# Linear attention and a SwiGLU layer on one core: tokens dealt in runs of five and four, v cast by DMA, another order in the prologue

## The chip, the cores and the metric

The kernel runs on one core of a Trainium2 chip. The metric is device time in microseconds, and lower is better. TensorE (PE in the profile, PEld for its weight loads) multiplies matrices; VectorE (DVE), ScalarE (ACT) and GpSimd (POOL) do the elementwise work; SyncE (SP) only issues transfers. DMAs go out on the queues of SP (q1 in the profile), ACT (q10) and POOL (q0). Only those of POOL change the type on the way, here from float32 to bfloat16. PSUM is the memory that matmuls write; DVE and ACT copy results out of it.

## The reference, cut to what matters

There are 8 batches of 8 heads, 576 tokens and a head dimension of 64.

```python
kv  = einsum('bhsd,bhse->bhde', k, v)
out = einsum('bhsd,bhde->bhse', q, kv)
a   = out / sqrt(mean(out*out, -1) + 1e-6) * g_norm
x   = a.transpose(0, 2, 1, 3).reshape(4608, 512)
xn  = x / sqrt(mean(x*x, -1) + 1e-6) * rms_g
y   = (silu(xn @ w_gate) * (xn @ w_val)) @ w_out     # 512 -> 1536 -> 512
```

## The kernel before, in words

**Tokens.** The 576 tokens of a batch are cut into 512 "main" tokens and 64 "remainder" tokens (`REM`). Main token `4p + c` lies on partition `p`, in chunk `c` (0 to 3, `NC = 4`). The remainder is a chunk number 4 of its own, on partitions 0 to 63 only. So q, k and v of a batch each take a main load (`load_main`, 1 MB, 128 partitions, pieces of 1024 bytes) and a remainder load (`load_rem`, 128 KB, 64 partitions, pieces of 256 bytes), and each is cast to bfloat16 in a main part (`cast_main`, two halves of heads, H0 and H1) and a remainder part (`cast_rem`, tiles `remq`, `remk`, `remv`). The remainder tokens of all batches are gathered in `xr` and go through the feed-forward layer last, as a ninth group. Heads go in pairs `j` (0 to 3, `NS = 4`), two heads filling 128 rows; P0 is pairs 0 and 1, P1 is pairs 2 and 3.

**Attention.** `kv_mm` or `kv_pairs` (L237, L247) accumulates k-transpose times v over the five chunks; `kv_out` copies it to `kvs`. `qT_mm` (L267) transposes q on TensorE and `qT_out` (L277) copies it out to `qTs` (batches 0 and 1); later batches do it by DMA (`qT_dma`). `oT_mm` (L324) and `sqT_` (L335) give the squared output transposed, and `stat_pairs` or `stat_mm` (L343, L353) its sums. `chain` is a row of twelve small DVE instructions (L381 to L399) that folds both norms into one factor per token and head; `xna_` (L307, L409) applies it, `xT_mm` (L426) transposes the result on TensorE, and `xT_out` copies it out as `x`, by turns on DVE (L438) and ACT (L436).

**Feed-forward.** For a group `g`, `slots_a` makes a "gate" and a "val" slot for each of 12 columns `j` of `d_ff` (L536, four matmuls of 128x512 each), and `slots_b` makes 16 slots of three matmuls (L558) for the output projection. Batch 0 uses `slots_b_by_j`, with four PSUM tiles open at once. `store` copies the result out of PSUM (`osb`, L575) and writes it to HBM.

**Order.** Each engine executes its instructions in the order in which the program emits them. `Placer` hands the attention work of the next batch to the slots of the batch before it: `put` takes the first slot from a given one on in which a table of room per engine (`ROOM`, `BEHIND`) is not overrun, and an operation whose input is made by another engine goes at least one slot later. In `emit`, a slot's work for the other engines comes ahead of its matmuls, and its attention matmuls behind them. Slots are numbered from the gate of column 6 of batch 0: 0 to 11 are the rest of `slots_a(0)`, 12 to 27 the "all" slots of `slots_b_by_j(0)`, and 28 to 33 are six empty ones, which hold only what the planner puts there; batch 1's feed-forward begins at slot 34. Attention of batch 1 is placed from slot 10 on, its kv first, then its qT.

**Prologue.** Batch 0's attention is written out by hand. v comes by casting DMAs of POOL in three pieces; k on SP and q on ACT in halves of heads; the three remainders on ACT and SP, behind them. The weight loads on POOL have a manual dependence on the first v load. Batch 1's loads on SP are held until the third `wg` load has landed, and batch 2's until the last `wo` load has. The tile framework orders two engines that read the same PSUM tile one behind the other.

The functions that the diff touches, with the profile's line numbers:

Of the kernel before, what the change touches and what calls it, by code (L numbers as in the profile page):

```python
# [80 lines left out]
def kernel(  # L81
# [32 lines left out]
    rstage = pool("rstage", 4)  # L114
# [17 lines left out]
    gcol = consts.tile([128, 1], FP32, name="gcol")  # L132
    rmsg = consts.tile([128, NS], FP32, name="rmsg")
# [11 lines left out]
    for t in range(3):  # L145
        nc.vector.memset(rems[t][0][REM:], 0.0)
    nc.vector.memset(kvs[0], 0.0)
# [6 lines left out]
    staged, rstaged = {}, {}  # L154
    mains, xs = {}, {}

    def load_main(b, t, heads=(0, H), cs=(0, NC), queue=nc.sync):
        if (b, t) not in staged:
            staged[b, t] = stage.tile([128, H, NC * D], FP32, name="stg")
        h0, h1 = heads  # L160
        view = src[t][b, :, 0:MAIN, :].rearrange("h (p c) d -> p h (c d)", c=NC)
        return queue.dma_start(  # L162
            out=staged[b, t][:, h0:h1, cs[0] * D : cs[1] * D], in_=view[:, h0:h1, cs[0] * D : cs[1] * D]
        )

    def by_head(t):
        if (0, t) not in mains:
            mains[0, t] = qkv.tile([128, NC, H, D], BF16, name=f"main_{'qkv'[t]}")
        return mains[0, t].rearrange("p c h d -> p (c h d)").rearrange("p (h x) -> p h x", h=H)

    def load_cast(t, heads):
        h0, h1 = heads
        view = src[t][0, :, 0:MAIN, :].rearrange("h (p c) d -> p h (c d)", c=NC)
        return nc.gpsimd.dma_start(out=by_head(t)[:, h0:h1], in_=view[:, h0:h1])

    def load_rem(b, t, queue=nc.sync):
        rstaged[b, t] = rstage.tile([REM, H, D], FP32, name="rstg")
        return queue.dma_start(out=rstaged[b, t], in_=src[t][b, :, MAIN:S, :].rearrange("h p d -> p h d"))

    def cast_main(b, t, eng, heads=(0, H), cs=(0, NC)):  # L180
        if (b, t) not in mains:
            mains[b, t] = qkv.tile([128, NC, H, D], BF16, name=f"main_{'qkv'[t]}")
        h0, h1 = heads
        copy = eng.copy if eng is nc.scalar else eng.tensor_copy
        copy(  # L185
            out=mains[b, t][:, cs[0] : cs[1], h0:h1, :],
            in_=staged[b, t].rearrange("p h (c d) -> p c h d", c=NC)[:, cs[0] : cs[1], h0:h1, :],
        )

    def cast_rem(b, t, eng):  # L190
        copy = eng.copy if eng is nc.scalar else eng.tensor_copy
        copy(out=rems[t][b % 2][:REM], in_=rstaged[b, t])

    def load_all(b):
        first = None
        for t in (0, 1, 2):
            i = load_main(b, t)
            first = first or i
        for t in (0, 1, 2):
            load_rem(b, t)  # L200
        return first
# [11 lines left out]
    class Att:  # L213
        def __init__(self, b):
            self.b = b
            self.kv, self.qT = kvs[b % 2], qTs[b % 2]
            self.o, self.outa, self.sq = {}, {}, {}
# [3 lines left out]
        def chunk(self, t, c):  # L221
            if c == NC:
                return rems[t][self.b % 2]
            if self.b == 0 and t == 2:
                return by_head(t).rearrange("p h (c d) -> p c h d", c=NC)[:, c]
            return mains[self.b, t][:, c]
# [46 lines left out]
        def qT_out(self, ps, js, c0, eng):  # L273
            copy = eng.copy if eng is nc.scalar else eng.tensor_copy
            n = ps.shape[2] // 128
            to = self.qT[:, c0 : c0 + n, js[0] : js[-1] + 1, :].rearrange("p c j t -> p j c t")
# [8 lines left out]
        def o_mm(self, c, pool=None):  # L285
            self.o[c] = o = (pool or att_p).tile([128, H, D], FP32, name={None: "att"}.get(pool, "mm1" if pool is mm1_p else "o2"))
            for j in range(NS):
                nc.tensor.matmul(  # L288
                    o[:, 2 * j : 2 * j + 2, :], lhsT=self.qT[:, c, j, :], rhs=self.kv[:, j, :, :],
# [3 lines left out]
        def o_pairs(self, js, c0, c1, pool, name):  # L293
            o = pool.tile([128, c1 - c0, 2 * len(js), D], FP32, name=name)
            for n, c in enumerate(range(c0, c1)):
                for i, j in enumerate(js):
                    nc.tensor.matmul(
                        o[:, n, 2 * i : 2 * i + 2, :], lhsT=self.qT[:, c, j, :], rhs=self.kv[:, j, :, :],
# [21 lines left out]
        def oT_mm(self, js, c0, c1, pool=None):  # L320

            ps = (pool or att_p).tile([128, len(js), (c1 - c0) * 128], FP32, name="o2" if pool else "att")
            for n, j in enumerate(js):
                nc.tensor.matmul(  # L324
                    ps[:, n], lhsT=self.kv[:, j], rhs=self.qT[:, c0:c1, j, :],
# [87 lines left out]
        def x_to(self):  # L413
            if self.b not in xs:
                xs[self.b] = x_p.tile([128, NC, NS, 128], BF16, name="x")
# [16 lines left out]
        def xT_out(self, j, chunks, eng):  # L432
# [9 lines left out]
            if chunks[0] < NC:  # L442
                copy(
                    out=self.x_to()[:, chunks[0] : chunks[-1] + 1, j, :],
# [27 lines left out]
    def place_attention(P, b, casts=(), at=0, chain_at=0, by_pe=False):  # L472
# [7 lines left out]
        p0 = P.psum(0.57, lambda: a.kv_mm((0, 1)), casts)  # L480
        p1 = P.reads(P.put("PE", 0.57, lambda: a.kv_mm((2, 3)), [p0], at=p0[1]))
        kv = [P.reads(P.put("DVE", 0.4, lambda h=h: a.kv_out(h, V), [p1])) for h in range(2)]
        ps = {}
        if by_pe:
            qt = []
            for j in range(NS):
                p = P.psum(0.29, lambda j=j: ps.__setitem__(j, a.qT_mm((j,), N1)), casts)
                eng = ("DVE", V) if j % 2 == 0 else ("ACT", A)
                qt.append(P.reads(P.put(eng[0], 0.67, lambda j=j, e=eng[1]: a.qT_out(ps[j], (j,), 0, e), [p])))
        outs = {}  # L490
# [38 lines left out]
    def x_of(g, s, c0, c1):  # L529
        return xs[g][:, c0 // 128 : c1 // 128, s, :] if g < B else xr[:, s, c0:c1]  # L530
# [31 lines left out]
    def rows_of(g, t):  # L562

        if g < B:
            view = out[g * S : g * S + MAIN, :].rearrange("(p c) d -> p c d", c=NC)
            return [(slice(0, 128), view[:, t, :])]
        return [
            (slice(n * REM, (n + 1) * REM), out[b * S + MAIN : (b + 1) * S, :])
            for n, b in enumerate((2 * t, 2 * t + 1))
        ]  # L570
# [33 lines left out]
    def slots_b_by_j(g):  # L604
# [4 lines left out]
        def part(n):  # L609
# [6 lines left out]
            if n == 4 * PARTS - 1:  # L616
                for t in range(4):
                    store(g, t, box[t], nc.scalar if t % 2 else nc.vector)
# [18 lines left out]
    v_load = [load_cast(2, hsx) for hsx in (H0, (4, 6), (6, 8))][0]  # L637
    load_main(0, 1, H0)
    load_main(0, 0, H0, queue=A)
    load_main(0, 1, H1)  # L640
    load_rem(0, 1, A)
    load_main(0, 0, H1, queue=A)
    load_rem(0, 2, A)
    load_rem(0, 0)
    A.preload_act_table(ACT.Silu)
    with nc.allow_non_contiguous_dma(reason="one column of gains"):
        for half in range(2):
            nc.sync.dma_start(out=gcol[half * D : (half + 1) * D], in_=g_norm.rearrange("(d o) -> d o", o=1))
        nc.sync.dma_start(out=rmsg, in_=moe_rms_g.rearrange("(s p) -> p s", p=128))
    nc.sync.dma_start(out=gbc, in_=g_norm.partition_broadcast(128))  # L650

    make_identity(nc, ident)
    w_loads = [load_w(n) for n in range(len(FB))]
    tc.add_manual_dep(w_loads[0][0].ins, v_load.ins.name, SYNC, reason="the first batch comes first")
    for t in range(3):
        G.memset(rems[t][1][REM:], 0.0)
    G.memset(kvs[1], 0.0)
# [10 lines left out]
    cast_rem(0, 1, V)  # L668
    cast_rem(0, 2, V)
    ps = a.qT_mm(P0, range(NC))  # L670
    a.qT_out(ps[:, 0:1], (0,), 0, A)
    a.qT_out(ps[:, 1:2], (1,), 0, V)
    kva = a.kv_pairs(P0)
    a.kv_pairs_out(kva, P0, 0, V)
    a.kv_pairs_out(kva, P0, 1, A)
    cast_main(0, 0, A, H1)
    cast_main(0, 1, V, H1)
    ps = a.qT_mm(P1, range(NC))
    a.qT_out(ps[:, 1:2], (3,), 0, V)
    t0 = a.oT_mm((0,), 0, NC, o2_p)  # L680
    a.sqT_(t0, (0,), 0, NC)
    a.qT_out(ps[:, 0:1], (2,), 0, A)
    t1 = a.oT_mm((1,), 0, NC, o2_p)
    cast_rem(0, 0, V)
    a.sqT_(t1, (1,), 0, NC)
    ps = a.qT_mm(ALL, (NC,))
    a.qT_out(ps, ALL, NC, A)
# [3 lines left out]
    for j in ALL:  # L691
        V.scalar_tensor_tensor(
            out=gain[:, j : j + 1], in0=rmsg[:, j : j + 1], scalar=float(d_model) ** 0.5, in1=gcol,
# [127 lines left out]
```

## Time and profile before

| what | value |
|---|---|
| median of 3 runs | 347.32 us (346.94 to 347.33) |
| the profiled execution | 346.48 us, of which the span is 344.7 us |
| busy PE, DVE, ACT, POOL | 317.0, 177.3, 136.2, 101.9 us |
| instructions | 4872 |
| DMA moved | 49.38 MB in 77336 packets, 43392 of them under 512 bytes |
| HBM read, written | 37.78 MB, 9.44 MB |

The profile is one execution. It lists busy time by engine and by groups of instructions, what ended each wait, the chain of work that ended last, a timeline, and busy time by chosen stretches. A matmul's busy time holds the latency of its result, so that neighbours overlap; the pace is read from their starts. In rows of stretches the count of instructions stands in brackets, and the last columns are the granted TensorE clock (1.00 is full), the busy share of the DMA engines and the bytes written by DMA in GB/s. A casting DMA counts there with its bfloat16 bytes.

### The profile page before, as it was taken

To read this page: it belongs to the slowest core of one execution; us is meant where nothing else is said; L and a number is where in the kernel's file an instruction comes from. 1 tells how busy PE (TensorE), PEld (TensorE's weight loads), DVE (VectorE), ACT (ScalarE), POOL (GpSimd) and SP (SyncE) were. 2 spreads that over 40 slices of the span, in tenths; PEclk is the share of its full clock that TensorE was granted. 3 is DMA by queue.
4 is the path that set the end of the run, shared out by engine and by line. 5 is a ranking of instruction groups with operands and counts; after the bars stand their busy time and mean duration, and the time that the engine had idled before them with its cause. 6 is when DMAs were issued, how large, how long until landed. Compare 5 with 4: busy or idle time off the path is not lost.

```text
span 344.7 us, 4872 instructions
## 1 busy us (share of the span) xinstructions
PE 317.0 (92%) x1776; PEld 159.0 (46%) x1776; DVE 177.3 (51%) x381; ACT 136.2 (40%) x247; POOL 101.9 (30%) x118
## 2 busy tenths in 40 slices
PE   1187999969899999999999999999999999999993
PEld 1155646545344544554455445444544444444441
DVE  2236534466993678076817671965296423303310
ACT  1142333425953742274228323732473233223321
POOL 3711913503920590068007700860150000000000
PEclk9999999969999999999999999999999999999999
DMA  8999989179606890698259645954200510020013
GB/s 220 212 205 310 242 141 368 32 192 341 132 8 160 281 224 21 164 330 167 48 150 335 139 75 156 350 92 99 91 2 1 128 65 0 0 108 16 0 32 92
DMA packets 77336, 49.38 MB, mean 143 GB/s; under 512 B 43392, under 2 KB 72832, under 8 KB 77312
## 3 DMA queue, kind: packets, MB, share of 16 engines
q1 hardware_dynamic: 69200, 42.38, 44.9%
q0 software_dynamic: 5840, 5.24, 9.5%
q10 hardware_dynamic: 2272, 1.44, 1.5%
q8 instruction: 14, 0.23, 0.3%
q14 instruction: 10, 0.08, 0.1%
HBM read 37.78 MB, written 9.44 MB: 137 GB/s over the span
## 4 chain that ended last, share of the span: by engine, by line
PE 85%; DVE 6%; DMA 4%; ACT 2%; issue 1%; ACTq 1%; POOL 0%; DVEq 0%
PE mm L536 52%; PE o L558 24%; DMA rstg<-in_v_dram 3%; PE att L237 3%; PE att L288 2%; PE mm L558 1%; DVE st L364 1%; DVE xna L409 1%; PE att L324 1%; DVE wg L663 1%; DVE h L553 1%; ACT sqT L335 1%; PE att L267 1%; DMA out_dram<-osb 1%; ACTq L162 0%
## 5 line engine op out<-in xcount | busy, mean ns | idle before, releaser
L553 DVE TENSOR_TENSOR h<-silu,mm 128x512 bf16<-128x512 bf16 (+1 forms) x111 | 74.3, 670 | 80.5 <-PE mm L536 69.8
L547 ACT ACTIVATE silu<-mm 128x512 bf16<-128x512 f32 (+1 forms) x111 | 65.1, 587 | 96.0 <-PE mm L536 85.0
L536 PE MATMUL mm<-x,wg 128*128 128x512 bf16 (+1 forms) x396 | 101.1, 377 | 1.1 <-DVE h L553 1.1
L536 PE MATMUL mm<-x,wv 128*128 128x512 bf16 (+1 forms) x396 | 99.5, 374 | 0.0
L558 PE MATMUL o<-wo,h 128*128 128x512 bf16 x408 | 92.6, 379 | 0.0
L536 PEld LDWEIGHTS <-wg 128*128 128x128 bf16 x444 | 43.7, 99 | 51.7 <-issue 2.7
L359 POOL TENSOR_TENSOR sq<-sq,g 128x512 bf16<-128x512 bf16 x30 | 34.4, 1153 | 101.6 <-ACT sq L314 101.4
L558 PEld LDWEIGHTS <-h 128*128 128x128 bf16 x432 | 41.7, 98 | 47.8 <-DVE h L553 0.2
L536 PEld LDWEIGHTS <-wv 128*128 128x128 bf16 x444 | 42.5, 98 | 44.6 <-issue 0.3
L575 ACT COPY osb<-o 128x512 f32<-128x512 f32 x32 | 18.8, 587 | 72.1 <-PE o L558 72.1
L364 DVE TENSOR_REDUCE st<-sq 128x8 f32<-128x512 bf16 x60 | 38.4, 677 | 0.0
L261 DVE CAST kvs<-att 64x256 bf16<-64x256 f32 x14 | 5.9, 421 | 40.7 <-PE att L237 40.6
L185 POOL CAST main_q<-stg 128x1024 bf16<-128x1024 f32 x14 | 14.4, 1040 | 40.7 <-DMA stg<-in_q_dram 24.5
L409 DVE TENSOR_TENSOR xna<-outa,al 128x512 bf16<-128x512 bf16 x35 | 21.8, 684 | 0.0
L318 ACT CAST outa<-att 128x512 bf16<-128x512 f32 x32 | 19.0, 594 | 0.9 <-PE att L288 0.9
L314 ACT ACTIVATE sq<-att 128x512 bf16<-128x512 f32 x30 | 18.2, 606 | 0.0
L185 POOL CAST main_k<-stg 128x1024 bf16<-128x1024 f32 x14 | 14.3, 1043 | 2.7 <-PE att L324 2.0
L185 POOL CAST main_v<-stg 128x1024 bf16<-128x1024 f32 x14 | 14.2, 1047 | 1.6 <-DMA stg<-in_v_dram 1.6
L536 PE MATMUL mm<-xr,wv 128*128 128x512 bf16 x48 | 12.3, 379 | 0.0
L536 PE MATMUL mm<-xr,wg 128*128 128x512 bf16 x48 | 12.3, 379 | 0.0
L288 PEld LDWEIGHTS <-qTs 128*128 128x128 bf16 x140 | 9.7, 98 | 5.3
L267 PE MATMUL att<-ident,main_q 128*128 128x128 bf16 x32 | 3.5, 265 | 8.9 <-DVE main_q L185 7.1
(96 smaller groups left out, 179.4 us busy)
## 6 DMA issues: line engine op xcount, KB each, us to landing
out_dram<-osb SPq DMA_DIRECT2D x32, 256.0 KB, 2.5
stg<-in_q_dram SPq DMA_DIRECT2D x7, 1024.0 KB, 6.5
stg<-in_k_dram SPq DMA_DIRECT2D x7, 1024.0 KB, 9.0
stg<-in_v_dram SPq DMA_DIRECT2D x7, 1024.0 KB, 11.9
wo<-in_moe_w_out_dram POOLq DMA_DIRECT2D x4, 384.0 KB, 7.4
stg<-in_k_dram SPq DMA_DIRECT2D x2, 512.0 KB, 6.5
stg<-in_q_dram ACTq DMA_DIRECT2D x2, 512.0 KB, 8.6
rstg<-in_q_dram SPq DMA_DIRECT2D x8, 128.0 KB, 10.3
```

Source lines behind the costliest of these rows:

```text
L185: copy(out=mains[b, t][:, cs[0] : cs[1], h0:h1, :], in_=staged[b, t].rearrange("p h (c d) -> p c h d", c=NC)[:, cs[0] : cs[1], h0:h1, :],)
L288: nc.tensor.matmul(o[:, 2 * j : 2 * j + 2, :], lhsT=self.qT[:, c, j, :], rhs=self.kv[:, j, :, :], start=j == 0, stop=j == NS - 1, skip_gro ...
L314: nc.scalar.activation(out=self.sq[c][:, 0], in_=self.o[c], func=ACT.Square)
L318: (eng.tensor_copy if eng else nc.scalar.copy)(out=self.outa[c], in_=self.o[c])
L359: eng.tensor_tensor(out=self.sq[c][:, 1], in0=self.sq[c][:, 0], in1=g2, op=OP.mult)
L364: nc.vector.reduce_sum(out=self.st[:, which, c, :], in_=self.sq[c][:, which], axis=AX.X)
L409: eng.tensor_tensor(out=self.xna[:, c], in0=src, in1=self.al[:, c, :].to_broadcast([128, H, D]), op=OP.mult)
L536: nc.tensor.matmul(ps[:, : c1 - c0], lhsT=w[n][:, s, jj * 128 : (jj + 1) * 128], rhs=x_of(g, s, c0, c1), start=s == 0, stop=s == NS - 1)
L547: nc.scalar.activation(out=si, in_=g_ps, func=ACT.Silu)
L553: nc.vector.tensor_tensor(out=hs[g, j][:, c0:c1], in0=box["silu"], in1=v_ps, op=OP.mult)
L558: nc.tensor.matmul(ps, lhsT=hs[g, j][:, t * 128 : (t + 1) * 128], rhs=wo[j // OB][:, j % OB, :], start=j == 0, stop=j == NF - 1)
L575: (eng.copy if eng is nc.scalar else eng.tensor_copy)(out=o, in_=ps)
```

## The change

Tokens are now dealt otherwise. A batch's 576 tokens go in 128 runs: partition `p` below 64 takes the five tokens from `9p` on, partition `64 + p` the four that follow. The fifth token of the lower half is chunk 4. So one tile holds main and remainder, and each load is two DMAs, one for each half of the partitions (pieces of 1280 and 1024 bytes); the remainder loads and their tiles are gone. `rows_of` follows: a store of batches 0 to 7 is two DMAs of 64 partitions, where it was one of 128. v of batches 0 and 1 goes by casting DMA into a tile `v01`. The prologue does P0 up to its squares before it casts the second half of the heads. The gain vectors come as rows, in three small DMAs on ACT's queue, and are transposed on TensorE. The weight loads no longer wait for the v load. `qTs` of batches 0 and 1 is stored by head pair. Attention of batch 1 is placed from slot 3 on, qT first, kv from slot 9, and the empty slots are two. Batch 3's loads and casts are asked for six slots later, and the four copies of `slots_b_by_j`'s store are all ACT's. The core of the diff:

```diff
+    v01 = consts.tile([128, H, (NC + 1) * D], BF16, name="v01")
...
-    for t in range(3):
+    for t in range(2):
         nc.vector.memset(rems[t][0][REM:], 0.0)
+    nc.vector.memset(v01[REM:, :, NC * D :], 0.0)
...
+    def runs(t, b, heads):
+        view = src[t][b].rearrange("h (p r) d -> p h r d", r=2 * NC + 1)[:, heads[0] : heads[1]]
+        return view[:, :, 0 : NC + 1], view[:, :, NC + 1 :]
+
+    def load(b, t, heads=(0, H), queue=nc.sync):
...
+        for n, of in enumerate(runs(t, b, heads)):
+            to = staged[b, t][n * REM : (n + 1) * REM, heads[0] : heads[1], : of.shape[2] * D]
+            i = queue.dma_start(out=to, in_=of.rearrange("p h r d -> p h (r d)"))
...
+    def load_v01(b, heads=(0, H)):
+        for n, of in enumerate(runs(2, b, heads)):
+            to = v01[n * REM : (n + 1) * REM, heads[0] : heads[1], : of.shape[2] * D]
+            nc.gpsimd.dma_start(out=to, in_=of.rearrange("p h r d -> p h (r d)"))
...
     def load_all(b):
...
+        return [load(b, t) for t in range(3 if b > 1 else 2)][0]
...
+            if b < 2:
+                self.qTj = self.qT.rearrange("p c j t -> p (c j t)").rearrange("p (j c t) -> p j c t", j=NS, c=NC + 1)
...
-                xs[self.b] = x_p.tile([128, NC, NS, 128], BF16, name="x")
+                x = x_p.tile([128, NC, NS, 128], BF16, name="x")
+                if self.b < 2:
+                    x = x.rearrange("p c j t -> p (c j t)").rearrange("p (j c t) -> p c j t", j=NS, c=NC)
+                xs[self.b] = x
...
-                    out=self.x_to()[:, chunks[0] : chunks[-1] + 1, j, :],
+                    out=self.x_to()[:, j, chunks[0] : chunks[-1] + 1, :],
...
+        return xs[g][:, s, cs, :] if g < 2 else xs[g][:, cs, s, :]
...
-    v_load = [load_cast(2, hsx) for hsx in (H0, (4, 6), (6, 8))][0]
...
+    for hsx in (H0, H1):
+        load_v01(0, hsx)
+    load(0, 1, H0)
+    load(0, 0, H0, queue=A)
+    load(0, 1, H1)
+    load(0, 0, H1, queue=A)
     A.preload_act_table(ACT.Silu)
...
     make_identity(nc, ident)
+    make_identity(nc, identf)
     w_loads = [load_w(n) for n in range(len(FB))]
-    tc.add_manual_dep(w_loads[0][0].ins, v_load.ins.name, SYNC, reason="the first batch comes first")
     for t in range(3):
         G.memset(rems[t][1][REM:], 0.0)
+        if t:
+            G.memset(rems[t][0][REM:], 0.0)
     G.memset(kvs[1], 0.0)
...
     cast_main(0, 0, V, H0)
     cast_main(0, 1, V, H0)
-    cast_rem(0, 1, V)
-    cast_rem(0, 2, V)
+    cast_rem(0, 0, V, H0)
+    cast_rem(0, 1, V, H0)
     ps = a.qT_mm(P0, range(NC))
     a.qT_out(ps[:, 0:1], (0,), 0, A)
     a.qT_out(ps[:, 1:2], (1,), 0, V)
+    ps = a.qT_mm(P0, (NC,))
+    a.qT_out(ps, P0, NC, A)
     kva = a.kv_pairs(P0)
     a.kv_pairs_out(kva, P0, 0, V)
-    a.kv_pairs_out(kva, P0, 1, A)
+    a.kv_pairs_out(kva, P0, 1, V)
+    for j in P0:
+        tj = a.oT_mm((j,), 0, NC, o2_p)
+        a.sqT_(tj, (j,), 0, NC)
+    cast_main(0, 1, V, H1)
     cast_main(0, 0, A, H1)
-    cast_main(0, 1, V, H1)
+    cast_rem(0, 1, V, H1)
+    cast_rem(0, 0, V, H1)
     ps = a.qT_mm(P1, range(NC))
...
+    a.qT_out(ps[:, 0:1], (2,), 0, A)
     a.qT_out(ps[:, 1:2], (3,), 0, V)
...
+    ps = a.qT_mm(P1, (NC,))
+    a.qT_out(ps, P1, NC, A)
+    gT = o2_p.tile([128, NS + 1], FP32, name="o2")
+    nc.tensor.matmul(gT, lhsT=grow, rhs=identf, is_transpose=True, start=True, stop=True, skip_group_check=True)
+    V.tensor_copy(out=gall, in_=gT)
...
         V.tensor_tensor(out=sel[rows, 1, half : half + 1], in0=gcol[rows], in1=gcol[rows], op=OP.mult)
-    for j in ALL:
-        V.scalar_tensor_tensor(
...
+    V.tensor_scalar(
+        out=gain, in0=gall[:, 0:NS], scalar1=gcol, scalar2=float(d_model) ** 0.5, op0=OP.mult, op1=OP.mult
+    )
...
+    load_v01(1)
+    wo_loads = [load_wo(n) for n in range(NF // OB)]
...
-                    store(g, t, box[t], nc.scalar if t % 2 else nc.vector)
+                    store(g, t, box[t], nc.scalar)
...
-    slots += [Slot("all", lambda: None) for _ in range(6)]
+    slots += [Slot("all", lambda: None) for _ in range(2)]
...
-            end = place_attention(P, b, casts, 10, by_pe=True)
+            end = place_attention(P, b, casts, 3, by_pe=True, kv_at=9)
...
-            P.put("SP", 0.0, lambda b=b: load_all(b + 1), at=starts[b - 1])
-            casts = place_casts(P, b + 1, starts[b - 1] + 5)
+            P.put("SP", 0.0, lambda b=b: load_all(b + 1), at=starts[b - 1] + 6 * (b == 2))
+            casts = place_casts(P, b + 1, starts[b - 1] + 5 + 6 * (b == 2))
```

## The prediction

> **What bounds the kernel now.** The page comes first: PE is busy 317.0 of 344.7 us. The windows say where it is not. Columns: the stretch, its length, busy time of PE, PEld, DVE, ACT and POOL, granted clock, DMA share, GB/s.
>
> ```profile
> 0.00:14.80 14.80, 1.62 (x12) 1.30 (x13) 3.45 (x12) 1.87 (x2) 7.08 (x15) 1.00 1.00 219
> 14.80:36.00 21.20, 16.32 (x131) 11.63 (x131) 11.35 (x38) 8.75 (x19) 6.04 (x9) 1.00 1.18 261
> ...
> 65.00:77.00 12.00, 8.74 (x69) 5.09 (x68) 9.08 (x28) 2.86 (x6) 1.16 (x3) 0.73 0.52 138
> 77.00:100.40 23.40, 22.28 (x124) 10.94 (x123) 19.84 (x37) 15.87 (x31) 13.44 (x14) 0.99 0.62 178
> ...
> 133.70:167.00 33.30, 33.30 (x185) 16.34 (x184) 19.88 (x41) 14.27 (x26) 13.25 (x14) 1.00 0.65 175
> ```
>
> From 100 us on PE has no gap, so nothing there can be won; only a new wait could show. Time lies in the prologue, between 65 and 77 us, and a little (1.1 us) up to 100 us. The chain of waits names the prologue's first stretch:
>
> ```profile
> 3.18 11.07 DMA rstg<-in_v_dram
> 14.28 0.48 DVE remv L192
> 14.81 0.81 PE mm L247 x6
> 16.25 1.05 ACT main_q L185
> 17.34 1.03 PE att L267 x8
> ```
>
> v's remainder, last in ACT's queue, lands at 14.28; P0's kv, begun at 10.54 when v H0 landed, stands until then. The second stretch is the end of batch 1's attention, in the timelines of PE and, under it, of DVE:
>
> ```profile
> 65.22 0.64 PE L353 MATMUL att<-sel,sqT 128*128 128x4 bf16 x20
> 67.88 0.59 PE L558 MATMUL mm<-wo,h 128*128 128x512 bf16 x2
> 71.44 1.03 PE L426 MATMUL att<-ident,xna 128*128 128x128 bf16 x8 [1.57 <-DVE xna L409]
> 75.27 1.91 PE L536 MATMUL mm<-x,wg 128*128 128x512 bf16 x4
> ```
>
> ```profile
> 68.90 0.69 DVE L409 TENSOR_TENSOR xna<-outa,al 128x512 bf16<-128x512 bf16 x1
> 69.51 0.68 DVE L575 COPY osb<-o 128x512 f32<-128x512 f32 x1
> 70.11 0.68 DVE L575 COPY osb<-mm 128x512 f32<-128x512 f32 x1
> 70.71 1.88 DVE L409 TENSOR_TENSOR xna<-outa,al 128x512 bf16<-128x512 bf16 x3
> ```
>
> After the sums (L353) PE has four slots of output projection left, and is out of work at 68.5; chain, two `osb` copies, `xna` and the copies of x follow each other, and x is whole at 75.77, with PE at half clock.
>
> **Prologue, loads.** Let L be when v H0 is whole. Before, 10.54, in the same place at the head of POOL's queue. By then 2.35 MB had been written, 0.26 MB of them v H0: other queues took most of the traffic, so L in the changed kernel may be as late as when all of q and k (2.36 MB) and v H0 (0.30 MB in bfloat16) are in, 2.66 MB from 2.2 us on. What rate? Rows of the DMA by stretches (length, granted clock, DMA share, GB/s):
>
> ```profile
> 12.00:13.00 1.00, 1.00 1.45 208
> 32.00:34.00 2.00, 1.00 1.09 387
> 60.00:64.00 4.00, 1.00 0.45 88
> ```
>
> Mains on 128 partitions reach 387 GB/s (L = 9.1); a stretch of remainders, 64 partitions in 256-byte pieces, shows 88 (L = 32). The new loads have 64 partitions and big pieces. Rows between are nearer: 2.0 to 10.5 us, the mix of mains and remainders, had 283 GB/s (L = 11.6), and 7 to 13 us, where remainders and the gains' 4-byte pieces weighed most, 241 (L = 13.2). I take their mean, L = 12.4. What goes (24 remainder loads, 640 four-byte pieces) speaks for faster, what comes (every load on half the partitions) for slower.
>
> The page "SBUF — State Buffer" of the Trainium skill, section "Door 1: The DMA port swizzle", speaks against the change: 64 partitions reach half of the ports, 196 GB/s measured against 328, and two DMAs, one for each half, bring 6% more. By it an estimate of L would be 15.8 and the total some 3.4 us above my forecast; no row here shows big pieces on 64 partitions.
>
> **Prologue, from L to the chain.** Ten kv matmuls at this cold stretch's pitch of 0.11, 1.2 us with the last one's latency; two `kvs` copies, both DVE's, 0.28 each, 0.6; `oT` 0.6; two squares on ACT 1.1; then, queued behind them on ACT, the cast of q H1, 1.05; eight transposes 1.05; `qTs` on ACT 0.6 and on DVE 0.4 (one PSUM tile, so one after the other); the gains' copy, `sel` and `gain`, small DVE instructions, 0.75; two `kvs` copies 0.45. With a tenth for hand-overs, `oT` of pair 2 starts at L + 7.9. Before it started at 21.18, and what follows up to the chain (3.78 us, to 24.96) is the same instructions. So the break-even is L = 13.3, and L = 12.4 saves 0.9. k's remainder cast and v's are no more on this path; the halves of k and q land ahead of v H0 and hide behind it.
>
> A floor: `remk`'s zeros are written once more by POOL, and kv's fifth chunk reads them. POOL has four v issues (0.78 each) from 1.26, two identities (0.6), six weight issues (0.77) and three memsets (0.52) before: 11.7, as if L were 11.3. With the memset row of 1.24 us (L657's neighbour at 15.75) it is nearer 12. If the new memset of `v01` on DVE also holds the first v issue, up to 0.6 more. So the prologue saves at most 2.0.
>
> Weights: not held by v any more, but behind it in the same queue, so they start when v H1 ends, at about 13 to 16 us where it was 14; `wg`, `wv` of columns 3 to 5 are needed at 37, of column 6 at 42, and the last landed at 30.7. Covered by over 8 us; cover gone, each us costs one. The v load of batch 1 waits on POOL for P1's kv (about 20 us); queued behind it are the four `wo` issues and the casts of q and k. These had until 54 and now have until 45 (qT at slot 3), against casts of q done at 35.4. Nothing.
>
> **Batch 1's attention.** By the planner's rule qT takes slots 3, 3, 3, 5 (0.29 against 0.3 of room, 0.6 behind), kv slots 9 and 10 (10 and 11 before), `oT` starts at 12 instead of 16, the sums at 19 instead of 23. So four slots (12 matmuls at 0.215, 2.58 us) now lie behind the sums. From the sums' start, before: chain +0.69, first `xna` +3.68, x whole +10.55. After: DVE loses two `osb` copies (1.2 us), so the fourth `xna` ends at about +6.2, the fifth at +7.1; PE ends its slots and transposes at +7.5. ACT has the four `osb` copies (0.49 pitch) from +7.4 to +9.4, ahead of its two copies of x's second half; these alternate with DVE's on one PSUM tile (0.47, 0.35, 0.47): x is whole at +10.75. Saved: 2.58 - 0.2 = 2.4. Against it, batch 2's first kv (10 matmuls, 0.55) lay in the idle time and now lies in slot 32. The clock: PE stopped at 68.5, the granted clock was 0.50 from 71 to 77, and the first gate took 1.7 us instead of 0.86. Its gaps will now be 0.6 and 1.8 us; a full clock is worth 0.9, I count half. Sum 2.4 - 0.55 + 0.45 = 2.3, between 1.0 (clock lost for a slot more) and 4.0 (clock kept, and ACT's `osb` not in the way).
>
> "TensorE: Matmul & The Clock Gate", Part 1, puts the drop after an idle window of about 3.4 us that runs free of the kernel, while here 2.3 us of near idleness were followed by it; by the rule an estimate is that the clock keeps up as often as not.
>
> **Up to 100 us.** DVE's folds and sums (L663, L364) stop PE for 0.30 and 0.82 us. Attention of batch 2 now comes four slots later against the folds; between all 1.1 saved and 0.5 lost, I take 0.2 saved.
>
> **Later batches.** SP gets four more stores a group and slower loads. Batch by batch the last remainder cast is at 195.7 and the output it serves begins at 214.4; at 208 GB/s the loads (3.54 MB) take 17 us instead of 14, well inside. The order of SP's transposes of x (204.77) gets one more store issue (0.5) before it, of 2 us to spare. Zero; but a miss would count six times. POOL loses v's casts of batch 1. The tail is as it was.
>
> `qTs` by pair: the strided rows already moved at full pace (L324 at 0.21 a matmul), so nothing. x by pair does not happen: `xT_out` indexes j first in a view whose first axis is c, both of length four, and `x_of` likewise, so each value keeps its old address. Zero either way.
>
> **Sum.** 346.48 - 0.9 - 2.3 - 0.2 = 343.1 for the profiled execution. The median of the runs is 0.84 above it: 343.9.
>
> **Rivals.**
> 1. Slower: loads on half the partitions crawl. Each us of L beyond 13.3 costs one; with 2.5 won elsewhere it decides, by over 0.2% (0.7 us, about what a measurement can tell), from L = 16.5, which is 186 GB/s. At 160, L = 18.8 and the time 350.3. For it: the row of 88. Against: that row's pieces are small, and the last group's stores of 64 partitions take 2.3 us for 128 KB where 256 KB on 128 take 2.5. 0.15.
> 2. Loads are as good as the mains, L at or under the floor of 11.3: 2.0 saved, 342.8, and 340.6 if the clock holds too. 0.25.
> 3. Nothing to be told: L at 13.3, and the four slots given back to ACT's copies, kv and the clock (1.0 or less): 346.5. 0.10.
> My forecast has 0.50. Faster: 0.76 (forecast, rival 2, a little of 3), same 0.08, slower 0.16. The range: 340.6 from below; above, 208 GB/s (L = 15.0, 1.7 lost) with the gap's 1.0 gives 348.0.
>
> **What would show it.** L247's first group waits for a DMA of `v01` until about 12.4 and for no remainder; if POOL's memset releases it, the floor is met. The chain's first instruction (L381) stands at 24.1. The sums of batch 1 come 2.6 us earlier against the first gate of column 6, x whole 10.75 after them. It is wrong if PE has gaps beyond 100 us, if weights are waited for, or if v lands beyond 15.

## The result, and the profile after

The changed kernel takes 357.15 us (median of 4 runs, 356.01 to 357.89) against 347.13 for the kernel before beside it: a ratio of 1.0293, 95% interval 1.0252 to 1.0334. It is slower by 10.0 us where 3.4 us faster was forecast, and above the forecast's range (340.6 to 348.0). The profiled execution took 356.52 us with a span of 354.7, against 346.48 and 344.7.

The page of the changed kernel, its row of PE and the shares of the chain of waits:

```profile
PE 318.2 (90%) x1777; PEld 157.6 (44%) x1777; DVE 185.2 (52%) x381; ACT 136.9 (39%) x247; POOL 103.1 (29%) x122
...
PE 63%; DVE 13%; DMA 11%; issue 3%; SPq 3%; ACT 3%; POOL 3%; DVEq 0%; POOLq 0%
```

PE has the same work to do (317.0 us before), but PE's share of the chain fell from 85% to 63%; DVE has 13% where it had 6, DMAs 11% where they had 4. The same stretches as before the change (length, busy PE, PEld, DVE, ACT, POOL, granted clock, DMA share, GB/s):

```profile
0.00:14.80 14.80, 1.83 (x16) 1.55 (x17) 3.33 (x12) 2.14 (x3) 9.70 (x22) 1.00 0.97 206
14.80:36.00 21.20, 15.37 (x110) 10.41 (x109) 10.45 (x35) 7.09 (x14) 5.63 (x9) 1.00 1.24 217
65.00:77.00 12.00, 9.14 (x65) 4.24 (x62) 8.76 (x25) 4.15 (x9) 6.38 (x7) 1.00 0.53 109
77.00:100.40 23.40, 22.71 (x135) 11.33 (x134) 15.40 (x29) 16.88 (x32) 9.34 (x9) 1.00 1.02 206
133.70:167.00 33.30, 31.74 (x176) 15.33 (x175) 21.12 (x41) 13.68 (x25) 13.37 (x14) 1.00 0.78 166
```

The last row is what counts: 33.3 us in the middle of the kernel, in which PE had no gap before, now have 1.6 us of them. The groups of batches 2 to 5 take 35.1 to 36.1 us instead of 33.3, that of batch 1 is longer too; those of batches 6 and 7, beside which no batch is loaded any more, are as before.

**The prologue.** PE's timeline at P0's kv, then POOL's:

```profile
12.23 0.63 PE L242 MATMUL mm<-v,main_k 128*128 128x128 bf16 x4
14.64 0.29 PE L242 MATMUL mm<-v,remk 128*128 128x128 bf16 x1 [1.77 <-POOL remk L653]
```

```profile
12.36 0.74 POOL L199 DMA_DIRECT2D wv<-in_moe_w_val_dram  x1 [3.87 <-DMA v<-in_v_dram]
13.14 0.52 POOL L651 MEMSET remq<- 64x512 bf16 x1
13.60 0.52 POOL L651 MEMSET remk<- 64x512 bf16 x1
14.07 0.52 POOL L653 MEMSET remk<- 64x512 bf16 x1
```

v H0 was whole at 12.1 (12.4 forecast), and kv begins at 12.23, right behind the transposes of q, without a wait for a load. But the fifth chunk of kv waited 1.8 us for `remk`'s second zeros: POOL's tenth DMA issue stood 3.87 us until a load of v had landed, and the zeros are queued behind it. The chain starts at 25.87 where it started at 24.96.

**A middle group.** POOL of the kernel before, then of the changed kernel, in the group that begins at 144.44 and at 148.62:

```profile
151.84 1.15 POOL L359 TENSOR_TENSOR sq<-sq,g 128x512 bf16<-128x512 bf16 x1 [0.62 <-ACT sq L314]
152.94 1.03 POOL L185 CAST main_q<-stg 128x1024 bf16<-128x1024 f32 x1
153.94 1.16 POOL L359 TENSOR_TENSOR sq<-sq,g 128x512 bf16<-128x512 bf16 x1
```

```profile
156.02 1.15 POOL L354 TENSOR_TENSOR sq<-sq,g 128x512 bf16<-128x512 bf16 x1 [0.62 <-ACT sq L309]
159.57 1.04 POOL L183 CAST main_q<-stg 128x1024 bf16<-128x1024 f32 x1 [2.40 <-DMA stg<-in_q_dram]
160.57 2.27 POOL L354 TENSOR_TENSOR sq<-sq,g 128x512 bf16<-128x512 bf16 x2
164.76 2.02 POOL L183 CAST main_k<-stg 128x1024 bf16<-128x1024 f32 x2 [0.95 <-DMA stg<-in_k_dram]
169.87 2.06 POOL L183 CAST main_v<-stg 128x1024 bf16<-128x1024 f32 x2 [3.09 <-DMA stg<-in_v_dram]
```

The order is the same: a cast of the next batch's q stands between the squares of this batch's attention. Before, the cast found its data there: q was issued 1.20 us after the group's head and landed after 6.0, at 151.7. Now q's second DMA is issued 2.71 us after the head and lands after 8.1, at 159.5; the cast waits 2.40 us, and the squares behind it with it. DVE and PE of the changed kernel show who waits for the squares:

```profile
161.75 0.69 DVE L359 TENSOR_REDUCE st<-sq 128x8 f32<-128x512 bf16 x1 [1.21 <-POOL sq L354]
162.36 0.68 DVE L555 TENSOR_TENSOR h<-silu,mm 128x512 bf16<-128x512 bf16 x1
...
171.03 0.94 DVE L385 TENSOR_SCALAR y<-z 128x40 int32<-128x40 int32 x1
172.01 0.53 DVE L392 TENSOR_TENSOR nt<-y 128x40 f32<-128x40 f32 x1
172.57 0.52 DVE L393 TENSOR_TENSOR nt<-nt,z 128x40 f32<-128x40 f32 x1
173.02 0.68 DVE L555 TENSOR_TENSOR h<-silu,mm 128x512 bf16<-128x512 bf16 x1
```

```profile
163.09 1.02 PE L538 MATMUL mm<-x,wg 128*128 128x512 bf16 x4 [0.54 <-DVE h L555]
...
175.16 7.51 PE L560 MATMUL o<-wo,h 128*128 128x512 bf16 x34 [0.85 <-DVE h L555]
```

The first gap: `h` is queued on DVE behind the sum that waits for the square, and its PSUM tile comes free late. By matmul starts it costs 0.71 us (163.09, and 162.38 by the pitch of 0.215). The second costs 1.01 and comes from v: its casts begin at 169.87, those of the remainders follow, and both run beside DVE's chain. Instructions of that chain that took 0.18 and 0.20 in the kernel before (165.61 to 166.06 there) take 0.94, 0.53 and 0.52, and the last `h`, queued behind them, is late for the output projection. Together 1.7 of the 1.8 us by which this group is longer.

### The profile page after: what moved, and what is told of

The parts are those of the page before. It is cut to its first block, busy times and chain, and to the rows that moved or that the text cites. A ratio compares the mean times of both kernels' runs of the same rounds, so it can differ in the third digit from the quotient of the medians.

```text
span 354.7 us, 4921 instructions
## 1 busy us (share of the span) xinstructions
PE 318.2 (90%) x1777; PEld 157.6 (44%) x1777; DVE 185.2 (52%) x381; ACT 136.9 (39%) x247; POOL 103.1 (29%) x122
## 4 chain that ended last, share of the span: by engine, by line
PE 63%; DVE 13%; DMA 11%; issue 3%; SPq 3%; ACT 3%; POOL 3%; DVEq 0%; POOLq 0%
PE mm L538 37%; PE o L560 20%; DMA stg<-in_q_dram 4%; DVE h L555 4%; DMA stg<-in_k_dram 3%; DMA v<-in_v_dram 3%; PE att L232 2%; SPq L576 1%; PE att L283 1%; DVE nt L392 1%; DVE y L385 1%; ACT osb L574 1%; DVE z L382 1%; POOL sq L354 1%; DVE xna L404 1%
## 5 line engine op out<-in xcount | busy, mean ns | idle before, releaser
L256 DVE CAST kvs<-att 64x256 bf16<-64x256 f32 x14 | 5.9, 421 | 35.0 <-PE att L232 34.9
L404 DVE TENSOR_TENSOR xna<-outa,al 128x512 bf16<-128x512 bf16 x35 | 23.2, 726 | 0.1
L183 POOL CAST main_q<-stg 128x1024 bf16<-128x1024 f32 x14 | 14.4, 1038 | 23.9 <-DMA stg<-in_q_dram 21.7
L183 POOL CAST main_v<-stg 128x1024 bf16<-128x1024 f32 x12 | 12.8, 1097 | 15.2 <-DMA stg<-in_v_dram 12.0
L262 PE MATMUL att<-ident,main_q 128*128 128x128 bf16 x32 | 3.4, 265 | 12.9 <-DVE main_q L183 11.2
```

The source lines that it names most:

```text
L183: copy(out=mains[b, t][:, cs[0] : cs[1], h0:h1, :], in_=staged[b, t].rearrange("p h (c d) -> p c h d", c=NC + 1)[:, cs[0] : cs[1], h0:h1, :],)
L404: eng.tensor_tensor(out=self.xna[:, c], in0=src, in1=self.al[:, c, :].to_broadcast([128, H, D]), op=OP.mult)
```

## The experiments

The kernels, from their profiled executions in us: the start of batch 1's sums, the head (first gate) of batch 2's group, the mean of the three groups from there on, and the span. At head 2, kernels whose medians agree can be 1.4 us apart (2 and 4), so a smaller difference of two single executions there says little. Then come the median and the ratio to the kernel before with its interval (its median beside them was 346.75 to 347.13).

| kernel | sums | head 2 | group | span | median | ratio |
|---|---|---|---|---|---|---|
| before | 65.22 | 111.13 | 33.31 | 344.7 | 347.13 | 1 |
| changed | 64.66 | 113.46 | 35.44 | 354.7 | 357.15 | 1.0293 [1.0252, 1.0334] |
| 2: changed, old dealing from batch 2 | 64.22 | 109.89 | 33.32 | 343.1 | 345.49 | 0.9963 [0.9940, 0.9986] |
| 3: before, new dealing from batch 2 | 65.16 | 114.74 | 35.34 | 356.7 | 359.01 | 1.0325 [1.0274, 1.0377] |
| 4: as 2, stores in halves | 63.38 | 111.31 | 33.32 | 344.4 | 345.76 | 0.9971 [0.9951, 0.9991] |
| 5: as 2, loads later | 63.17 | 110.27 | 34.38 | 348.4 | 352.24 | 1.0143 [1.0113, 1.0172] |
| 6: changed, loads earlier | 63.64 | 117.16 | 34.26 | 354.3 | 354.22 | 1.0197 [1.0165, 1.0228] |
| 7: changed, casts later | 62.86 | 114.70 | 37.81 | 364.3 | 367.23 | 1.0610 [1.0574, 1.0646] |
| 8: changed, no second zeros | 62.47 | 113.03 | 35.52 | 354.4 | 356.12 | 1.0275 [1.0210, 1.0341] |
| 9: as 2, no second zeros | 62.15 | 110.79 | 33.32 | 343.9 | 345.56 | 0.9960 [0.9939, 0.9982] |
| 10: old dealing everywhere, no second zeros | 61.31 | 109.36 | 33.32 | 342.6 | 344.04 | 0.9905 [0.9880, 0.9931] |
| 11: before, slots of batch 1 alone | 62.82 | 109.16 | 33.31 | 342.6 | 344.09 | 0.9922 [0.9899, 0.9944] |
| 12: as 10, casts of batch 2's v by ACT | 61.19 | 108.83 | 33.31 | 342.1 | 342.42 | 0.9880 [0.9856, 0.9903] |

**1. The loads by themselves.** Six ways to load a batch, one after the other: mains and remainders; lower half, then upper, on SP; the halves on SP and ACT; halves in pieces of two heads by turns; the same two DMAs on alternate partitions; mains alone.

```python
return tile_[n * 64 : (n + 1) * 64, hs, : of.shape[2]]          # ways 2 to 4: where half n goes
...
nc.sync.dma_start(out=tile_[n:128:2, :, : of.shape[2]], in_=of)     # way 5
```

> Computes nothing: six stages, each the q, k and v of one batch (3.54 MB, the first and the last as named) loaded into three tiles, each stage held until the one before has landed. Stage 1: mains on 128 partitions, then remainders of 256-byte pieces. Stage 2: lower half of the partitions (1280-byte pieces), then upper half (1024), all on SP's queue, as in the changed kernel. Stage 3: the same, lower halves on SP's queue and upper halves on ACT's at once. Stage 4: as 2, but in pieces of two heads, lower and upper by turns. Stage 5: as 2, but the five-token runs on the even partitions and the four-token runs on the odd ones. Stage 6: mains alone. Theory A (64 neighbouring partitions reach only half of what takes writes in SBUF): stage 2 at about 220 GB/s, stages 3 and 5 well above it, 300 or more, stage 6 at 385. Theory B (two DMAs of 64 partitions are slow as such, by their count or by their pieces): 2, 3 and 5 all near 220. Theory C (something else in the kernel slows the loads, such as stores, POOL or PE): stage 2 alone runs at 350 or more.

Rows of 2 us, two each of the second way, the third and the fifth; none of them has stores in it:

```profile
24.00:26.00 2.00, 0.00 (x0) 0.00 (x0) 1.00 1.12 219
28.00:30.00 2.00, 0.00 (x0) 0.00 (x0) 1.00 1.10 218
...
42.00:44.00 2.00, 0.00 (x0) 0.00 (x0) 1.00 1.10 237
46.00:48.00 2.00, 0.00 (x0) 0.00 (x0) 1.00 1.09 341
...
78.00:80.00 2.00, 0.00 (x0) 0.00 (x0) 1.00 1.06 382
82.00:84.00 2.00, 0.00 (x0) 0.00 (x0) 1.00 1.08 361
```

DMAs of the same count, sizes and pieces take 218 to 222 GB/s into 64 neighbouring partitions and 356 to 382 into 64 alternate ones; mains on 128 take 335 to 378. The busy share of the DMA engines is as high in both (1.06 to 1.13), so a piece takes longer in the first. The third way, halves on two queues, had 234 to 255 GB/s from 40 to 46 us, in which the packets of SP's queue and of ACT's mostly moved by turns, and 341 to 343 from 46 to 52, in which both moved at once. The fourth way stayed at a DMA share of 0.8, held by SP's issues (eight take 5.2 us), and tells nothing. So theory A holds: it is which partitions are written at a time, not how many DMAs or pieces. Alternate partitions and two queues, which are fast by themselves, were not tried in the kernel.

**2 and 3. The dealing from batch 2 on, undone in the changed kernel and done alone in the kernel before.**

```diff
     def runs(t, b, heads):
+        if b >= DEAL4:      # 2 in kernel 2; its stores likewise; kernel 3 does the reverse in the kernel before
+            hs_ = slice(*heads)
+            return (
+                src[t][b][hs_, 0:MAIN].rearrange("h (p c) d -> p h c d", c=NC),
+                src[t][b][hs_, MAIN:S].rearrange("h (p o) d -> p h o d", o=1),
+            )
```

> The changed kernel, with batches 2 to 7 dealt as before (main on 128 partitions, remainder on 64, stores of 128 partitions); batches 0 and 1, the prologue and the planner's slots stay as changed. Theory A (loads on half the partitions run at 220 GB/s, POOL's casts wait for them, POOL's squares queue behind the casts, DVE's sums behind those, and PE at last): the groups from batch 2 on take 33.3 us again instead of 35.1 and the time is 346 to 347, 10 to 11 below the changed kernel. Rival (the new order in the prologue and of the slots is what costs, or the stores and SP's longer list, whatever the dealing of the inputs): under 3 us come back, 354 or more.

> The kernel before, with only the dealing of batches 2 to 7 changed: loads in runs of five and four on two halves of the partitions, stores in two halves, no remainder loads for them. Prologue, planner and batches 0 and 1 are as before. Theory A: the groups from batch 2 on grow from 33.3 to about 35 us, the whole to 355 to 357. Rival (the dealing costs only together with the new order of slots): within 2 us of the kernel before.

Theory A in both: the price comes and goes with the dealing of the later batches: 354.7 to 343.1 us of span without it, 344.7 to 356.7 with it alone. Groups are 33.31 to 33.33, and PE gapless in them, or 34.9 to 36.2.

**4. Loads or stores?** The new dealing also doubles the stores.

```diff
-            return [(slice(0, 128), out[g * S : g * S + MAIN, :].rearrange("(p c) d -> p c d", c=NC)[:, t, :])]
+            rows = out[g * S : g * S + MAIN, :].rearrange("(p c) d -> p c d", c=NC)[:, t, :]
+            return [(slice(n * REM, (n + 1) * REM), rows[n * REM : (n + 1) * REM]) for n in range(2)]
```

> The old dealing from batch 2 on, as in the kernel that came to 345.5, but every output tile of batches 2 to 7 is stored by two DMAs of 64 partitions, as in the changed kernel. Theory (the later loads of 64 neighbouring partitions are what costs): 345.5, between 344.6 and 346.5, groups of 33.3. Rival (twice as many stores hold the SP queue, and with it the transposes of x and the loads behind them): groups of 34 and more, 350 or above.

345.76: beside the fast loads, halved stores cost nothing that can be told (the intervals of 2 and 4 are nearly the same). 4 and the changed kernel (357.15) differ in how the later batches are loaded and in which rows a store writes, so it is the loads. Whole stores beside the slow loads were not tried.

**5. Lateness or traffic?** Fast loads of the old dealing, held back.

```diff
-    P.put("SP", 0.0, lambda b=b: load_all(b + 1), at=starts[b - 1] + 6 * (b == 2))
+    P.put("SP", 0.0, lambda b=b: load_later(b + 1), at=starts[b - 1] + 4 + 2 * (b == 2))
...
+    def load_later(b):      # h of column 1 of the running group
+        tc.add_manual_dep(load_all(b).ins, h_done[b - 2, 1].ins.name, SYNC, reason="later")
```

> The old dealing from batch 2 on, fast loads, but those of batches 3 to 7 are held until h of column 1 of the group before is done, some 2.9 us later than they began; this is how late q and k land in the changed kernel. Theory (it is the lateness: POOL's cast of q waits, the squares wait behind it on POOL, DVE's sums behind these, PE behind DVE's h; and v's casts run beside DVE's chain): gaps of PE before the gates in the first half of each group and at the first output projections, groups of 34.3 to 36, total 351 to 358. Rival (not the time of landing but something else of the new dealing, such as the traffic on half of the partitions itself): groups of 33.3, 345.5.

They began 5.66 us after the head of the group (144.53 to 150.19), 4.5 and not 2.9 later than in 2, since that `h` was done later than I took it. The same gap is there, in POOL's and PE's timelines:

```profile
155.76 1.04 POOL L196 CAST main_q<-stg 128x1024 bf16<-128x1024 f32 x1 [2.68 <-DMA stg<-in_q_dram]
```

```profile
159.28 1.02 PE L554 MATMUL mm<-x,wg 128*128 128x512 bf16 x4 [0.83 <-DVE h L571]
```

Groups of 34.3 to 34.5, one gap in each: with fast loads v and the remainders are cast by 166.5, ahead of most of the chain (165.4 to 169.2), and the second gap, expected too, is missing. So lateness alone makes the first gap, at the loads' old rate. The total, 352.24, is in the expected range.

**6. The loads earlier.**

```diff
-            P.put("SP", 0.0, lambda b=b: load_all(b + 1), at=starts[b - 1] + 6 * (b == 2))
+            P.put("SP", 0.0, lambda b=b: load_all(b + 1), at=starts[b - 1] - 4 + 6 * (b == 2))
```

> The changed kernel, with the loads of batches 3 to 7 issued four slots (some 3.5 us) earlier, between the second and the third of the four output tiles of the group before. Theory (lateness is the price): q lands before POOL comes to its cast, the gaps go, groups of 33.3 to 34, total 346 to 349. Rival (slow loads collide with something wherever they stand, here with the transposes of x or the stores): the gate at the head of each group waits for x or a store, groups of 35 or more, 355 or above.

Neither came true. The slots asked for were 3.5 us earlier, but SP came to the load at 151.87 with the group's head at 151.03, 0.84 after it where it was 1.97: SP's queue stands behind the transposes of x until then. One us of lateness less took away the first gap; the second stayed:

```profile
176.84 3.41 PE L560 MATMUL o<-wo,h 128*128 128x512 bf16 x15 [0.88 <-DVE h L555]
```

Groups fell to 34.26. In the first group, where the loads were not earlier at all (81.33 against 81.66), the wait before the output projection grew from 1.89 to 2.72 us and the granted clock fell behind it (0.72 from 106 to 112 us; 1.00 in the changed kernel there), so that the span of this execution, the slowest of four, gained next to nothing. The median, 354.22, is 2.9 us below the changed kernel's. With 5, the two gaps are seen apart: the first alone costs 1.1 us a group (34.38 against 33.32), the second alone 0.9 (34.26).

**7. The casts later.**

```diff
-    casts = place_casts(P, b + 1, starts[b - 1] + 5 + 6 * (b == 2))
+    casts = place_casts(P, b + 1, starts[b - 1] + 16 + 6 * (b == 2))
```

> The changed kernel with its dealing and its slow loads, but POOL's casts of batches 3 to 7 asked for from the 16th slot of the batch before on, and not from the 5th, so that its multiplications of squares (sq by g) stand ahead of them in its queue. Theory A (the load rate costs only through what is queued behind the casts): the PE gaps of 0.4 to 0.5 us in the middle of the gate and val slots, where DVE waits for POOL's squares, go; the second gap of each group (0.85 to 1.0, at the first output projections), where POOL casts v beside DVE's chain and stretches its small instructions from 0.2 to 0.9, stays. Some 2 to 3 us back, 354 to 355. Rival (transposes or the copies of x are late because the queue of SP is full): nothing comes back, 357.

A miss, and a costly one. The squares were now ahead of the casts, the first gap went and the second stayed (0.57 to 1.17 us), as theory A has it. But casts that end late delay q's transposes on SP, which come between the two of x. SP's timeline, then PE's at the head of the next group:

```profile
143.02 1.80 SPq L455 DMA_TRANSPOSE x<-xna  x1
144.94 1.62 SPq L276 DMA_TRANSPOSE qTs<-main_q  x1
147.09 1.18 SPq L278 DMA_TRANSPOSE qTs<-remq  x1
148.38 1.18 SPq L576 DMA_DIRECT2D out_dram<-osb  x2
149.66 1.31 SPq L455 DMA_TRANSPOSE x<-xna  x1
```

```profile
152.94 1.04 PE L538 MATMUL mm<-x,wg 128*128 128x512 bf16 x4 [2.38 <-DMA x<-xna]
```

**8 and 9. Without POOL's second zeros**, with the new and with the old dealing from batch 2 on.

```diff
-        if t:
+        if t == 2:
             G.memset(rems[t][0][REM:], 0.0)
```

> The changed kernel without POOL's second writing of remk's zeros (DVE has written them at the start). Theory (POOL reaches that memset late, held at its tenth DMA issue by the landing of v, and the fifth chunk of P0's kv stands from 13.3 to 14.6 for it): P0's kv ends 1.3 to 2 us earlier, the chain starts at 24.0 to 24.6 instead of 25.9, and the total falls by 1.3 to 2, to 355 to 356. Rival (the prologue is bound by the late halves of q and k): the chain stays at 25.9, the total at 357.

> The changed kernel with the old dealing from batch 2 on and without POOL's second zeros of remk. Theory: the two effects are apart and add: chain of batch 0 at 23.5 to 24 us, groups of 33.3 us, 343.5 to 344.5, faster than the kernel before by 2.5 to 3.5. Rival (the prologue's gain is swallowed by the next wait, at batch 1's attention): 345.5, as with the old dealing alone.

The wait for POOL is gone and the prologue goes as the prediction had it: kv at 12.12, `oT` of pair 2 at 20.02, the chain at 23.80 (8). That is 2.07 us won over the changed kernel at the chain, and 2.19 at the sums of batch 1, but 0.43 at the head of batch 2's group. The total of 8, 356.12, is at the edge of what was expected. In 9 nothing is left against 2 (345.56 against 345.49): its theory missed and its rival held. One place where the gain goes is seen in 10 and 12.

**10 and 11. The old dealing everywhere, and batch 1's slots alone.**

```diff
+    DEAL4 = 0                                # 10, where 9 has 2: the old dealing for every batch
...
+            end = place_attention(P, b, casts, 3, by_pe=True, kv_at=9)      # 11, in the kernel before
+    slots += [Slot("all", lambda: None) for _ in range(2)]                  # 11
+                    store(g, t, box[t], nc.scalar)                          # 11
```

> As the one before it, with the old dealing also for batches 0 and 1 (mains on 128 partitions, remainders of 256-byte pieces behind them, v cast by DMA). Theory A says that in the prologue too 128 partitions load faster: the halves of q and k land at 7 to 8 us instead of 10.4, v's first half at 11 to 12; the rest of the path is the same, so 343 to 344.5. Rival (the small pieces of the remainders hold v's first half up): it lands at 13 or later and the time is 345 to 346.

> The kernel before with only the planner's part of the change: attention of batch 1 from slot 3, qT first, kv from slot 9, two empty slots, the four copies of batch 0's store on ACT, batch 3's loads and casts six slots later. Dealing, loads and prologue as before. Theory (the prediction's sum for this part): 2.3 us faster, 1.0 to 4.0, so 344.5 to 346; x of batch 1 whole 10.75 us after the sums began. Rival (ACT's copies give the four slots back): within 0.7 us of the kernel before.

The slots alone are worth 2.1 us of span and 2.85 of the medians (344.09 against 346.94 beside it). 10 comes to 344.04, within its theory's range and 1.5 below 9, with v's first half whole at 11.3. It has its sums 1.5 earlier than 11 and is no faster.

**12. ACT casts v and the remainders of batch 2.** From the sums to the head of batch 1's group 11 takes 8.0 us and 10 takes 9.7; POOL's casts of batch 2 come when their loads land, and sums that are earlier meet them.

```diff
-                ops[t] = P.put("POOL", 1.1, lambda t=t, hs=hs: cast_main(b, t, nc.gpsimd, hs), at=at + 3 * n)
+                by = ("ACT", nc.scalar) if b == 2 and t == 2 else ("POOL", nc.gpsimd)      # remainders likewise
+                ops[t] = P.put(by[0], 1.1, lambda t=t, hs=hs, e=by[1]: cast_main(b, t, e, hs), at=at + 3 * n * (b > 2))
```

> The old dealing everywhere, four slots fewer and no second zeros (344.0), with v and the remainders of batch 2 cast by ACT, idle from 60.5 to 69.4 there, instead of POOL. Theory (POOL's casts beside DVE's chain of batch 1 stretched its small instructions from 0.20 to 0.5 and 0.9 and took back 1.7 us of the prologue's gain): chain back to 0.2 an instruction, xna 1.7 earlier after the sums, 342.3, between 341.5 and 343.2. Rival (the chain's stretch costs nothing in the end, as x waits for ACT's copies anyway, or ACT's casts hold up its copies of x): 344.0 to 345.

The last factor also asks for the casts of batch 2 all at one slot, where they were three slots apart. POOL's casts in 10, from 62.15 to 65.9, DVE's timeline beside them, and DVE's in 12:

```profile
62.15 2.08 POOL L196 CAST main_v<-stg 128x1024 bf16<-128x1024 f32 x2 [1.44 <-DMA stg<-in_v_dram]
64.18 0.60 POOL L204 CAST remq<-stg 64x512 bf16<-64x512 f32 x1
64.74 0.60 POOL L204 CAST remk<-stg 64x512 bf16<-64x512 f32 x1
```

```profile
63.36 0.91 DVE L398 TENSOR_SCALAR y<-z 128x40 int32<-128x40 int32 x1
64.30 0.53 DVE L405 TENSOR_TENSOR nt<-y 128x40 f32<-128x40 f32 x1
64.87 0.52 DVE L406 TENSOR_TENSOR nt<-nt,z 128x40 f32<-128x40 f32 x1
```

```profile
63.24 0.18 DVE L398 TENSOR_SCALAR y<-z 128x40 int32<-128x40 int32 x1
63.46 0.20 DVE L405 TENSOR_TENSOR nt<-y 128x40 f32<-128x40 f32 x1
63.70 0.20 DVE L406 TENSOR_TENSOR nt<-nt,z 128x40 f32<-128x40 f32 x1
```

The chain of twelve takes 3.0 us instead of 4.7, and the stretch is shown to come from POOL. Each stretched instruction ends 0.04 to 0.05 us after a cast of POOL does (64.27 after 64.23, 64.83 after 64.78, 65.39 after 65.34), as if it had stood until then. Not every one is stretched: the chain's reciprocal, its reduction and the instruction between them, which reads PSUM, keep their 0.40 and 0.20 from 62.2 to 63.1, beside the first cast. The total is the lowest of all, 342.42, close to the 342.3 expected, but against 10 the intervals overlap, and the profiled executions differ by only 0.5 at batch 2's head: that the casts' move brings all of the 1.6 us between the medians is not shown. Both beat the kernel before and the changed one.

**The sum in spans:** before 344.7; slots -2.1 (11); prologue and dealing of batches 0 and 1 +0.5 (2 against 11); loads of the later batches +11.6 (changed against 2); 354.7. In medians, each less that of the kernel before beside it: -2.85, +1.28 and +11.59, together the 10.0 of the result.

## Why the prediction was wrong

**The step that failed** is "Later batches": "Zero; but a miss would count six times". It measured 11.6 us: 1.8 to 2.8 in each of four groups, and 3.6 up to the head of batch 2's, of which 1.7 is the wait before the output projection of batch 1's group (1.89 us against 0.20 in 2). It held the last remainder cast (195.7) against the output that it serves (214.4), 18.7 us of room, and asked whether the loads would end in time; they do. But the cast of q is not only work for the next batch. On POOL it stands in the middle of this batch's squares, and there the room was 1.3 us: the load was issued at 145.64, landed after 6.0, at 151.7, and the cast began at 152.94. In the changed kernel q's second DMA lands 3.6 us later after the group's head, 2.1 of them from the longer transfer and 1.5 from the later issue. The consumer that counted was the next instruction in the queue, not the reader of the data. The second gap is of the same kind: v's data are late for nobody who reads them, but their casts now fall beside DVE's chain. The wait for `main_q` in the sum of waits would not have told: POOL waited 24.5 us for q before, where nothing was behind it, and 21.7 after.

**Rival 1** had the mechanism, loads that crawl on half of the partitions, and the wrong place. It was priced through L, the landing of v H0, with 0.15; there it did not bite, since L was 12.1. The rate measured 223 to 234 GB/s from 156 to 162 us, near the 208 that the "Later batches" step allowed: the rate was right and its consequence was not.

"SBUF — State Buffer" of the Trainium skill, section "Door 1: The DMA port swizzle", was the rule against the change. The loads by themselves agree with it: 218 to 222 GB/s against 335 to 378. By its mapping alternate partitions reach every port, which agrees with the 356 to 382 of the fifth way. The 6% that the prediction quotes for two DMAs, one for each half, stand in the page's section "Can I just issue two DMAs to hit both halves?"; the third way, with 341 to 343 GB/s while both halves moved at once, goes far beyond them, and the measurement decides. The estimate of L by the page's rate, 15.8, did not come true.

**The prologue** was forecast at -0.9 and cost +0.9 at the chain. The path of 7.9 us from kv to `oT` of pair 2 held (8: 12.12 and 20.02). L held too, in part by luck: the forecast's 2.66 MB in 10.2 us ask for 261 GB/s, while from 2.2 to 12.1 us the rate was 237, and only 2.35 MB were in; the last of q landed behind v H0, at 15.2, and not ahead of it. The term that was mis-sized is the floor: POOL's zeros at 11.7, which ended at 14.59. The terms listed for it add up to 11.2, one memset less than the 11.7 said, and POOL's instructions took no more (14.59 less the wait of 3.87 is 10.7); what was left out is that an issue could wait, here the tenth for v. From the chain to column 3 another 1.1 went: PE's four matmuls of 256 columns came every 0.85 us for 5.4 us from the first gate, where before it was 2.9.

**Batch 1's attention** held. The sums come 25.16 us after column 3's first gate where it was 27.74, 2.58 earlier. x is whole 10.5 us after the sums in 11 (10.75 forecast), and the net is 2.1 of span (2.3 and 0.2 forecast). In the changed kernel x is whole 11.35 after them, because POOL's casts of batch 2 run beside `xna`, four of which take 3.34 us and not 2.50. `qTs` by pair, which only batches 0 and 1 have, costs nothing that shows: a matmul that reads it in batch 1 is followed by the next after 0.21 us before (58.49 to 58.70) and after 0.22 now (57.92 to 58.14). The clock, of which the sum counted half, was kept in the changed kernel (1.00 from 65 to 77 us, 0.73 before) and fell again in 11 (0.50 from 75 to 77).

"It is wrong if PE has gaps beyond 100 us" was the right thing to look at. Two numbers of the sum do not come out as given, and neither decides anything: the row of 2.0 to 10.5 us reads 277 GB/s and not 283, which moves L by 0.1, and the lower end of the range, 340.6, would be 341.1 (342.8 less the 1.7 between 2.3 and 4.0).

## What to carry to other kernels

Before a transfer is made slower, find every instruction that waits for it and ask what stands behind that instruction in its queue; the room is that of the first one behind, and it is read as landing time against start. A step that is zero in one group is worth a second look for the number of its groups. When work is made earlier, look which engine beside it was idle until then and will now be casting.

## What was not expected of the hardware

- Loads into 64 neighbouring partitions, one after the other, run at 218 to 222 GB/s, into 64 alternate ones at 356 to 382, with DMAs of the same number, size and pieces. The two neighbouring halves, once both moved at the same time from two queues, had 341 to 343.
- Some small DVE instructions (128x40) take 0.5 to 0.9 us instead of 0.2 beside casts of POOL, until the cast ends, and 0.2 when ACT does the casts; others keep their time. "SBUF — State Buffer" of the Trainium skill, section "Who interferes with whom", has the rule that DVE and GpSimd share a pair of ports, which a DVE instruction needs if it has two SBUF inputs or runs in a 2-port mode and which one of the two holds for a whole instruction, while ACT has ports of its own; the runs agree as far as they show it.
- POOL's tenth DMA issue in the changed kernel stood 3.87 us until a load of its own queue had landed.
- After the idle stretch of the prologue PE runs at half its pace for 2.9 to 5.4 us, while the granted clock reads 1.00 in those rows. Why it was longer in some kernels stays open.
